# Moving two of sixteen attention numerators from a gate/up phase into the down phases

## The chip, the cores and the metric

The kernel runs on one core of a Trainium2 chip. The metric is device microseconds of one execution, lower is better. Times are medians; ratios are the mean time of one kernel's fast runs over that of the other's fast runs of the same rounds on the same chip, so they are not quite the ratio of the medians quoted beside them. All runs were at a granted TensorE clock of 0.999 or 1.0. The time from a DMA's issue to its last completion signal is called its *landing*.

## The reference, cut to what matters

```python
g = sigmoid((x * gate_w).sum(-1, keepdims=True))          # x: 2048 tokens x 640
# linear attention, 32 heads of 20
num = einsum("bhqf,bhfd->bhqd", phi_q, kv)                # "numerator" and, beside it, den
den = einsum("bhqf,bhf->bhq", phi_q, z)[..., None] + 1e-6
a = (num / den).reshape(B, S, D) @ wo
# GEGLU feed-forward, 640 -> 1728 -> 640
b = (gelu(x @ w_gate) * (x @ w_up)) @ w_down
out = g * a + (1 - g) * b
```

## The kernel before

Tokens are cut into 4 blocks of 4 tiles of 128. After the attention state (kv, z) is built, TensorE runs these phases in this order: gate/up of blocks 0 and 1, down of block 0, gate/up 2, down 1, gate/up 3, down 2, down 3. Each tile t also needs a *numerator*, `num(t)`: 20 small matmuls of TensorE into PSUM banks 2 to 5, ten VectorE operations, an add on GpSimd, and a DMA transpose into `goT`. The down phase then multiplies `goT` by `wo` in the same accumulation as the feed-forward. Every operation names ("marks") what it reads and writes, and the kernel's own scheduler makes a later writer wait for the last marked reader.

```python
def num(self, t):
    for i in range(self.KD):                  # 20 matmuls, two row halves r run side by side
        for s in (0, 1):
            for r in (0, 1):
                bk, a, o0 = NBK + 2 * r + s, 64 * r, 3 * i * DB          # NBK = 2
                sc.op("pe", lambda e: e.matmul(self.bank(bk)[:, o0:o0 + w], ...), writes=[("ps", bk)], ...)
    rb = [("ps", NBK + k) for k in range(4)]  # each VectorE operation that reads a bank marks all four as read
    dve(lambda e: e.reciprocal(R(0), Dn[1]), rb, [key(0)], guard=old)
    # ... seven more small operations ...
    for s, dst in ((0, self.O1), (1, self.O2)):
        dve(lambda e, ...: e.tensor_tensor(o, V[s][:, :, :, 0:DH], f, ALU.mult), rb + [key(6 + s)], ...)   # L678
    sc.op("pool", ... Og = O1 + O2 ...)                                   # L680
    sc.dma("sp", lambda e: e.dma_start_transpose(self.goT[:, gs, :, :], self.Og[:, sl, :]), ...)   # L683

# one down phase: two pairs of tiles, 74 steps each; a step is two matmuls (L708) that run side by side
cs = list(range(NFC + 1 if opens else NFC)) + [NFC + 1 + k for k in range(KD)]   # hT chunks, then goT chunks

def first_nums(idx):                          # second block's gate/up phase
    if idx in (2, 5, 8, 11):
        self.num(idx // 3)
at = (12, 46, 80, 116)                        # steps of a down phase after which a numerator is put
gateups(0, state)
gateups(1, first_nums)
for b in range(self.NB):
    downs(b, {at[k]: 4 * b + 4 + k for k in range(4)} if b < 3 else {})
    if b < 2:
        gateups(b + 2, none)
```

A pair needs its `goT` for the first time in step 15 of its 74, so the second pair of a phase needs it in step 89 of the phase.

The softmax here doesn't subtract the row's maximum and nothing guards it: scores larger than these inputs give would overflow.

Of the kernel before, what the change touches and what calls it, by code (L numbers as in the profile page):

```python
# [107 lines left out]
class _Kernel:  # L108
# [641 lines left out]
    def ffn(self):  # L750
        self.gn = 0
        self.pn = 0
        pairs = [(0, 1), (6, 7)]

        def gateups(b, after):
            for idx, c in enumerate([0, 1, 13] + list(range(2, 13))):
                self.gateup(b, c, pairs[self.pn % 2])
                self.pn += 1
                after(idx)

        def downs(b, side):
            p = [pairs[(self.pn + k) % 2] for k in (0, 1)]
            n = 0
            for t in (4 * b, 4 * b + 2):
                final = t + 2 == self.NT
                for _ in self.down_pair(t, p + [(2, 3)] if final else p, (256, 256, 128) if final else (320, 320)):
                    n += 1
                    if n in side:
                        self.num(side[n])

        def state(idx):
            if idx < 3:
                self.gram(13 + idx)
            if idx == 2:
                self.columns = False
                self.kv_evac()
                self.gates()
                self.kv_ones()
            if 6 <= idx < 11:
                self.kv_mask(idx - 6)  # L780

        def first_nums(idx):
            if idx in (2, 5, 8, 11):
                self.num(idx // 3)

        def none(idx):
            pass
        at = (12, 46, 80, 116)
        gateups(0, state)
        gateups(1, first_nums)  # L790
        for b in range(self.NB):
            downs(b, {at[k]: 4 * b + 4 + k for k in range(4)} if b < 3 else {})
            if b < 2:
                gateups(b + 2, none)

# [43 lines left out]
```

## Time and profile before

The kernel before took 289.85 us median of six runs (289.48 to 290.26).

| reading | number | where it is read |
|---|---|---|
| span | 288.7 us | page |
| TensorE busy | 98% of the span | page |
| chain that ended last | 97% TensorE | page |
| longest TensorE or weight-load wait after 86 us | under 0.5 us | waits |

The page's first part, busy time, share of the span and instructions of each engine:

```profile
PE 284.0 (98%) x3032; PEld 190.1 (66%) x3032; DVE 166.7 (58%) x337; ACT 105.1 (36%) x199; POOL 27.6 (10%) x52
```

From 86 us on the chain that ended last is an unbroken row of matmuls. These are pieces of it (start, length, what). First the gate/up stretches, without numerators and then with the first two of the second block's four; after the dots, the beginning of the second down phase:

```profile
86.32 29.24 PE ps L351 x135
115.56 0.50 PE ps L651 x20
116.06 6.67 PE ps L351 x30
122.73 0.50 PE ps L651 x20
123.23 6.58 PE ps L351 x30
...
192.93 1.74 PE ps L708 x24
194.67 0.39 PE ps L651 x20
195.06 4.62 PE ps L708 x68
```

Read: L351 is a gate or up matmul, 29.24/135 = 0.2166 us each, L651 a numerator's matmul, L708 a down matmul. Thirty L351 should take 6.50 us and take 6.58 to 6.67 after a numerator, so in gate/up a numerator costs its own 0.50 and about 0.1 more; in a down phase it costs about 0.4.

The timeline of the third down phase shows two numerators in a row and the room between them (start, length, engine, line, what; in brackets the idle time before and who ended it):

```profile
245.53 0.56 PE L651 MATMUL ps<-KV,Eq 64*128 64x88 bf16 x20
246.28 0.36 DVE L667 RECIPROCAL RH<-ps 128x32 f32<-128x32 f32 x1 [1.59 <-PE ps L651]
248.34 1.55 DVE L678 TENSOR_TENSOR O<-ps,RH 128x640 bf16<-128x640 f32 x2
250.02 1.39 POOL L680 TENSOR_TENSOR Og<-O,O 128x640 bf16<-128x640 bf16 x1 [34.32 <-DVE O L678]
250.40 0.55 PEld L651 LDWEIGHTS ps<-KV,Eq 64*128 64x128 bf16 x20
```

Read: the first numerator's matmuls begin at 245.53, VectorE reads the banks until 248.34 + 1.55 = 249.89, and the next numerator's weights load at 250.40 with no idle time in front. There is 0.5 us to spare.

### The profile page before, as it was taken

What the parts mean: (1) busy time and instruction counts of PE and PEld (TensorE: products, weight loads), DVE (VectorE), ACT (ScalarE), POOL (GpSimd) and SP (SyncE); (2) the same over time, 40 slices, a digit from 0 to 9 for tenths busy, and PEclk for the clock granted to TensorE, in tenths of its full rate; (3) what the DMA queues carried; (4) which work ended last, traced back from release to release, by engine and by line L of the source; (5) the groups of instructions that cost most, each with busy time, mean ns of one, the idle gap of its engine ahead of it and who ended that gap; (6) DMA issues with size and microseconds to landing.
All of it is one profiled execution on the core that took longest, in us unless ns stands there. A gap on an engine that the chain in (4) does not pass through costs nothing.

```text
span 288.7 us, 7036 instructions
## 1 busy us (share of the span) xinstructions
PE 284.0 (98%) x3032; PEld 190.1 (66%) x3032; DVE 166.7 (58%) x337; ACT 105.1 (36%) x199; POOL 27.6 (10%) x52
## 2 busy tenths in 40 slices
PE   7999999999999999999999999999999999999996
PEld 4576689999994444444688744457764444777785
DVE  2338999999977553777776443326744232674001
ACT  2357897687663322322111332220132222022111
POOL 7000000000000000111113200001230000113000
DMA  8999994000002000011212120000312000031211
GB/s 225 217 192 293 361 356 119 0 2 2 0 2 48 0 0 0 3 25 31 25 37 70 28 66 0 3 0 15 80 25 68 0 2 0 2 92 26 70 49 49
DMA packets 36938, 18.68 MB, mean 65 GB/s; under 512 B 28970, under 2 KB 36394, under 8 KB 36906
## 3 DMA queue, kind: packets, MB, share of 16 engines
q1 hardware_dynamic: 36096, 17.86, 23.8%
q8 instruction: 24, 0.39, 0.6%
q10 hardware_dynamic: 810, 0.35, 0.5%
q14 instruction: 8, 0.07, 0.1%
HBM read 9.04 MB, written 2.62 MB: 40 GB/s over the span
## 4 chain that ended last, share of the span: by engine, by line
PE 97%; DMA 1%; ACT 1%; issue 0%; ACTq 0%
PE ps L351 61%; PE ps L708 28%; PE ps L651 2%; PE ps L363 2%; PE ps L449 2%; DMA xtok<-in_A_x_dram 1%; PE ps L331 1%; PE ps L290 1%; ACT Ek L413 0%; ACT Eq L518 0%; ACT outsb L721 0%; ACT gcol L416 0%; PE ps L313 0%; ACTq L42 0%
## 5 line engine op out<-in xcount | busy, mean ns | idle before, releaser
L708 PE MATMUL ps<-wd_sb,hT 64*128 64x320 bf16 (+2 forms) x918 | 67.6, 288 | 0.0
L625 DVE TENSOR_TENSOR hT<-ps,gl 128x512 bf16<-128x512 f32 x52 | 35.7, 690 | 55.1 <-PE ps L351 54.9
L351 PE MATMUL ps<-xT,wg_sb 128*128 128x512 bf16 (+1 forms) x270 | 64.9, 379 | 0.0
L351 PE MATMUL ps<-xT,wu_sb 128*128 128x512 bf16 (+1 forms) x270 | 64.8, 379 | 0.0
L623 ACT ACTIVATE gl<-ps 128x512 bf16<-128x512 f32 x52 | 30.9, 597 | 71.5 <-PE ps L351 64.9
L708 PEld LDWEIGHTS ps<-wd_sb,hT 64*128 64x128 bf16 x918 | 46.0, 94 | 13.2 <-ACT gl L623 0.8
L351 PEld LDWEIGHTS ps<-xT,wu_sb 128*128 128x128 bf16 (+1 forms) x270 | 26.5, 99 | 29.7 <-DVE hT L625 0.4
L680 POOL TENSOR_TENSOR Og<-O,O 128x640 bf16<-128x640 bf16 x16 | 22.3, 1395 | 237.3 <-DVE O L678 237.3
L351 PEld LDWEIGHTS ps<-xT,wg_sb 128*128 128x128 bf16 (+1 forms) x270 | 25.9, 99 | 28.7 <-issue 0.5
L351 PE MATMUL ps<-w,xT 128*64 128x512 bf16 (+6 forms) x400 | 42.1, 325 | 0.0
L721 ACT ACTIVATE outsb<-ps,Gm 128x320 bf16<-128x320 f32 (+2 forms) x31 | 14.6, 516 | 74.8 <-PE ps L708 74.8
L351 PEld LDWEIGHTS ps<-w,xT 128*64 128x64 bf16 (+1 forms) x400 | 35.9, 107 | 4.7
L708 PE MATMUL ps<-wo_sb,goT 64*128 64x320 bf16 (+2 forms) x340 | 28.2, 288 | 0.0
L351 PE MATMUL ps<-xT,wq 128*64 128x512 bf16 (+1 forms) x185 | 26.4, 380 | 0.3 <-ACT Eq L518 0.3
L433 DVE TENSOR_TENSOR Ek<-Ek,Dk 128x640 bf16<-128x640 bf16 x32 | 25.0, 821 | 0.5
L678 DVE TENSOR_TENSOR O<-ps,RH 128x640 bf16<-128x640 f32 x32 | 24.8, 815 | 0.0
L424 DVE TENSOR_REDUCE Dk<-Ek 128x64 f32<-128x1280 bf16 x16 | 23.7, 1478 | 0.2 <-ACT gcol L416 0.2
L518 ACT ACTIVATE Eq<-ps 128x512 bf16<-128x512 f32 x40 | 21.7, 604 | 1.1 <-PE ps L351 0.8
L413 ACT ACTIVATE Ek<-ps 128x640 bf16<-128x640 f32 x32 | 20.7, 702 | 3.5 <-PE ps L351 3.5
L708 PEld LDWEIGHTS ps<-wo_sb,goT 64*128 64x128 bf16 x340 | 17.7, 94 | 4.7
L351 PEld LDWEIGHTS ps<-xT,wq 128*64 128x64 bf16 (+1 forms) x185 | 15.3, 108 | 3.5 <-ACT Eq L518 0.8
L667 DVE RECIPROCAL RH<-ps 128x32 f32<-128x32 f32 x16 | 5.7, 358 | 18.3 <-PE ps L651 18.3
(65 smaller groups left out, 151.1 us busy)
## 6 DMA issues: line engine op xcount, KB each, us to landing
out_dram<-outsb SPq DMA_DIRECT2D x7, 320.0 KB, 2.4
wd_sb<-in_B_w_down_dram SPq DMA_DIRECT2D x1, 2080.0 KB, 13.6
wg_sb<-in_B_w_gate_dram SPq DMA_DIRECT2D x1, 1120.0 KB, 6.0
wu_sb<-in_B_w_up_dram SPq DMA_DIRECT2D x1, 1120.0 KB, 8.5
wg_sb<-in_B_w_gate_dram SPq DMA_DIRECT2D x1, 960.0 KB, 9.7
wu_sb<-in_B_w_up_dram SPq DMA_DIRECT2D x1, 960.0 KB, 10.2
w<-in_A_wqkv_dram SPq DMA_DIRECT2D x5, 160.0 KB, 4.4
wo_sb<-in_A_wo_dram SPq DMA_DIRECT2D x1, 800.0 KB, 9.4
```

Of the source, the lines that this page charges most:

```text
L351: self.sc.op("pe", lambda e: e.matmul(self.ps[a:z, bank * 512 + c0:bank * 512 + c0 + n], lhs[:, a:z], rhs, start=first, stop=fin), reads=r ...
L363: sc.op("pe", lambda e, c0=c0, n=n, bk=bk, col=col: e.matmul(self.bank(bk)[:, col:col + n], self.xT[:, kt, t * P:(t + 1) * P], self.w3[:, ...
L413: self.sc.op("act", lambda e, s=s, scale=scale: e.activation(self.Ek[:, se, s, :], self.ps[:, o:o + self.D], AF.Exp, scale=scale), reads=[ ...
L424: sc.op("dve", lambda e: e.tensor_reduce(self.Dk[:, se, 0, :].rearrange("p (s h) -> p s h", h=H), self.Ek[:, se, :, :].rearrange("p s (h d ...
L433: sc.op("dve", lambda e, v=v, r=r: e.tensor_tensor(v, v, r, ALU.mult), reads=[("Rk", se)], writes=[("Ek", se, s)])
L518: sc.op("act", lambda e, s=s, scale=scale: e.activation(self.Eq[:, s, i, b * self.BT:(b + 1) * self.BT], self.bank(bank), AF.Exp, scale=sc ...
L623: sc.op("act", lambda e: e.activation(self.gl[:, slot, :], self.bank(banks[0]), AF.Gelu_apprx_tanh), reads=[("ps", banks[0])], writes=[("g ...
L625: sc.op("dve", lambda e: e.tensor_tensor(hT[:, c, :], self.bank(banks[1]), self.gl[:, slot, :], ALU.mult), reads=[("ps", banks[1]), ("gl", ...
L678: dve(lambda e, o=o, f=f, s=s: e.tensor_tensor(o, V[s][:, :, :, 0:DH], f, ALU.mult), rb + [key(6 + s)], [("O", s, sl)], guard=old)
L680: sc.op("pool", lambda e: e.tensor_tensor(self.Og[:, sl, :], self.O1[:, sl, :], self.O2[:, sl, :], ALU.add), reads=[("O", 0, sl), ("O", 1, ...
L708: sc.op("pe", lambda e: e.matmul(self.bank(bk, w), lhs, rhs, start=opens and x == 0, stop=end and not opens, skip_group_check=True), reads ...
L721: sc.op("act", lambda e: e.activation(dst, self.bank(bk, w), AF.Copy, scale=g), reads=rd, writes=wr)
```

## The change

The idea is that TensorE pays less for a numerator in a down phase than in a gate/up phase, so the second gate/up phase keeps only the two that block 0's first pair needs; each down phase then begins with the two of its own second pair.

```diff
         def first_nums(idx):
-            if idx in (2, 5, 8, 11):
-                self.num(idx // 3)
+            if idx in (4, 8):
+                self.num(idx // 4 - 1)
 ...
-        at = (12, 46, 80, 116)
+        at = (1, 29, 62, 98)
         gateups(0, state)
         gateups(1, first_nums)
         for b in range(self.NB):
-            downs(b, {at[k]: 4 * b + 4 + k for k in range(4)} if b < 3 else {})
+            downs(b, {at[k]: 4 * b + 2 + k for k in range(4 if b < 3 else 2)})
```

## The prediction

> **What bounds the kernel.** TensorE is busy 98% of the 288.7 us span and the chain that ended last is 97% TensorE, at full granted clock; every other engine is under 60%. In the waits view no PE or PEld wait after 86 us exceeds 0.5 us. Only TensorE time, or a new TensorE stall, can move the total.
>
> **What moves.** A "numerator" is 20 small matmuls into PSUM banks 2 to 5, then 10 VectorE operations, a GpSimd add and a DMA transpose into goT. There are 16 before and after. Before: 4 in the second gate/up phase, 4 in each of the first three down phases. After: 2, then 4, 4, 4, 2 by down phase.
> In the chain by time, the second gate/up stretch 115.56 to 141.81 is 26.25 us for 110 matmuls; without numerators 135 matmuls take 29.24, so 23.83 are matmuls and a numerator costs 0.605 us there. A down phase of 148 steps takes 21.78 us with 4 numerators; a pair without any takes 10.05, two 20.10: 0.42 us each. Moving two saves about 0.4 us of TensorE.
>
> **What it adds: two tight waits in each down phase.** By the timeline a down step is 0.136 us, VectorE starts 0.75 us after the numerator's first matmul, its chain lasts 3.61, GpSimd starts 0.13 later and lasts 1.40, the transpose lands 2.6 after its issue. (The Trainium skill, "Perfetto Trace Analysis", section "DMA Instruction — HWDGE": the profiled window leaves out the data movement; the trace agrees: windows of 1.2 us, landings 2.6 to 4.4.)
> 1. Banks 2 to 5. Before, numerators are 34 to 36 steps apart; now first and second are 28 apart: 28 x 0.136 + 0.42 = 4.22 us, while the banks are released 0.75 + 3.61 + about 0.05 = 4.4 us after the first's first matmul (all ten VectorE operations mark all four banks as read). With the lost weight prefetch a stall of 0.2 to 0.35 us in four down phases: about +1.0. The last gate/up product ends 0.8 us into the phase; the chain wants VectorE at 0.89, so it should not add.
> 2. The second numerator's goT. It starts 4.57 us into the phase and lands at 4.57 + 0.75 + 3.61 + 0.13 + 1.40 + 0.06 + 2.6 = 13.1. It is needed after step 88: 11.95 + 3 x 0.42 + 0.2 = 13.4 in the first three phases (fits), but 11.95 + 2 x 0.42 + 0.2 = 13.0, less 0.13 of prefetch, in the last: stall of 0.1 to 0.3.
> Steps 62 and 98 follow by 33 and 36 and fit.
>
> **Sum.** 289.78 - 0.4 + 1.0 + 0.2 = 290.6 us; 8 in 10: 289.4 to 292.0. Faster by over 2%: 1%, within 2%: 97%, slower: 2%.
>
> **What would show it.** Second gate/up phase shorter by 1.2 us. First three down phases longer by the stall alone, 0.2 to 0.35 each; the pause sits just before the second numerator, put down to VectorE's L678. Last down phase longer by 0.84 plus stalls, with a short pause before the second pair's wo matmuls, put down to the goT DMA. PE busy falls by 0.4, span rises.
>
> **What would make it wrong.** If VectorE releases the banks early enough, or TensorE's queue absorbs 0.2 us, the result is 289.4. If the last gate/up product delays the first chain, the stall grows and pushes the goT landing past its deadline too: +1 us per phase, 292 or more. A transpose that meets an output transfer landed in 4.4 us instead of 2.6; if the second numerator's does, +1.5 us per phase.

## The result, and the profile after

The changed kernel took 290.78 us median (290.03 to 291.05, 6 runs) against 289.85; the ratio is 1.0029, 95% interval 1.0014 to 1.0045. It is slower by 0.3%, well under the 2% line but clear of noise.

TensorE did a little less, yet the span grew:

```profile
PE 283.7 (98%) x3032; PEld 185.6 (64%) x3032; DVE 167.1 (58%) x337; ACT 105.0 (36%) x199; POOL 27.6 (10%) x52
```

After 86 us the waits view of the changed kernel has three lines for TensorE that the kernel before has not (engine, line, waited for: total us, times, longest):

```profile
PEld ps L708 <- DMA goT<-Og: 1.4, 2, 0.8
PEld ps L651 <- DVE O L678: 1.2, 3, 0.4
...
PE ps L708 <- DMA goT<-Og: 0.8, 2, 0.5
```

Now the chain's second gate/up stretch has only two numerators, and 40 or 50 matmuls between:

```profile
86.14 33.56 PE ps L351 x155
119.70 0.50 PE ps L651 x20
120.19 8.74 PE ps L351 x40
128.93 0.50 PE ps L651 x20
129.43 10.91 PE ps L351 x50
```

The third down phase's first two numerators, to be laid beside the lines of before:

```profile
242.89 0.69 DVE L625 TENSOR_TENSOR hT<-ps,gl 128x512 bf16<-128x512 f32 x1 [1.47 <-PE ps L351]
242.93 0.56 PE L651 MATMUL ps<-KV,Eq 64*128 64x88 bf16 x20
243.68 0.36 DVE L667 RECIPROCAL RH<-ps 128x32 f32<-128x32 f32 x1
245.75 1.55 DVE L678 TENSOR_TENSOR O<-ps,RH 128x640 bf16<-128x640 f32 x2
247.35 0.43 PEld L651 LDWEIGHTS ps<-KV,Eq 64*128 64x128 bf16 x20 [0.40 <-DVE O L678]
247.43 1.39 POOL L680 TENSOR_TENSOR Og<-O,O 128x640 bf16<-128x640 bf16 x1 [35.28 <-DVE O L678]
```

Read: the last gate/up product ends at 243.58 and VectorE begins the numerator at 243.68, 0.75 us after its first matmul, as predicted; it leaves the banks at 245.75 + 1.55 = 247.30, and only at 247.35 can TensorE load the second numerator's weights. The pause of 0.40 us is there in the first three down phases.

In the last down phase the two longest pauses are for `goT`, once before the first pair's `wo` matmuls and once before the second pair's. The first was not predicted:

```profile
263.44 1.21 SPq L683 DMA_TRANSPOSE goT<-Og  x1
...
267.74 0.52 PEld L708 LDWEIGHTS ps<-wo_sb,goT 64*128 64x128 bf16 x9 [0.78 <-DMA goT<-Og]
...
278.33 0.44 PEld L708 LDWEIGHTS ps<-wo_sb,goT 64*128 64x128 bf16 x9 [0.64 <-DMA goT<-Og]
```

The transpose issued at 263.44 is numerator 13's, the fourth of the third down phase; it landed 4.3 us after its issue, where most land in 2.6.

The loading at the start varies from run to run by more than the effects here: in fourteen traces the last group of attention-state matmuls began anywhere between 84.7 and 86.2 us, though of all edits only the 30 small matmuls of e6, e9, e10 and e12 come before it. Why it moves was not looked into. So the experiments are judged by the stretches behind it, which repeat to about 0.02 us where no pause varies. Stretch A runs from the start of the last group of attention-state matmuls to the first down matmul (it holds the first two gate/up phases), B and C from one down phase's start to the next one's, D from the third down phase's start to the end of the last matmul, as the timeline's starting times give them:

| us | A | B | C | D | sum | ratio of times to before, 95% interval |
|---|---|---|---|---|---|---|
| before | 55.99 | 51.13 | 51.01 | 42.04 | 200.17 | |
| after | 54.70 | 51.26 | 51.26 | 44.35 | 201.57 | 1.0029 (1.0014 to 1.0045) |
| e1_banks | 54.70 | 51.02 | 51.02 | 43.96 | 200.70 | 1.0021 (1.0006 to 1.0037) |
| e2_late | 54.70 | 51.25 | 51.26 | 44.10 | 201.31 | 1.0035 (1.0020 to 1.0050) |
| e3_both | 54.70 | 51.02 | 51.02 | 43.93 | 200.67 | 1.0013 (0.9999 to 1.0027) |
| e4_gap34 | 54.70 | 51.53 | 51.48 | 45.30 | 203.01 | 1.0087 (1.0071 to 1.0102) |
| e5_early | 54.69 | 51.02 | 51.02 | 43.32 | 200.05 | 0.9993 (0.9979 to 1.0007) |
| e6_fetch | 54.70 | 52.65 | 52.87 | 45.17 | 205.40 | 1.0187 (1.0171 to 1.0204) |
| e7_last1 | 54.70 | 51.02 | 51.02 | 42.82 | 199.56 | 0.9988 (0.9970 to 1.0006) |
| e8_marks | 54.70 | 51.26 | 51.26 | 44.53 | 201.75 | 1.0046 (1.0031 to 1.0061) |
| e9_before_fetch | 55.99 | 51.12 | 51.02 | 42.04 | 200.17 | 1.0003 (0.9985 to 1.0021) |
| e10_last1_fetch | 54.70 | 52.19 | 52.24 | 43.75 | 202.88 | 1.0071 (1.0042 to 1.0100) |
| e11_three | 55.31 | 51.02 | 51.02 | 42.43 | 199.78 | 0.9978 (0.9962 to 0.9995) |
| e12_three_fetch | 55.31 | 51.02 | 51.02 | 42.43 | 199.77 | 0.9996 (0.9979 to 1.0013) |

### The profile page after: what moved, and what is told of

Same layout as the page of the kernel before. It is cut to its first block, busy times and chain, and to the rows that moved or that the text cites. A ratio compares the mean times of both kernels' runs of the same rounds, so it can differ in the third digit from the quotient of the medians.

```text
span 289.8 us, 7035 instructions
## 1 busy us (share of the span) xinstructions
PE 283.7 (98%) x3032; PEld 185.6 (64%) x3032; DVE 167.1 (58%) x337; ACT 105.0 (36%) x199; POOL 27.6 (10%) x52
## 4 chain that ended last, share of the span: by engine, by line
PE 80%; DVE 6%; DMA 5%; SPq 4%; issue 1%; POOL 1%; ACT 1%; DVEq 0%; POOLq 0%; ACTq 0%
PE ps L351 58%; PE ps L708 18%; DMA wqT<-in_A_wqkv_dram 3%; DVE O L678 2%; DMA goT<-Og 2%; PE ps L651 2%; PE ps L449 2%; SPq L224 1%; SPq L220 1%; POOL Og L680 1%; SPq L233 1%; DVE hT L625 1%; DVE RH L667 1%; DVE RH L672 1%; PE ps L331 1%
## 5 line engine op out<-in xcount | busy, mean ns | idle before, releaser
L708 PEld LDWEIGHTS ps<-wd_sb,hT 64*128 64x128 bf16 x918 | 44.0, 94 | 15.1 <-ACT gl L623 0.8
L708 PE MATMUL ps<-wo_sb,goT 64*128 64x320 bf16 (+2 forms) x340 | 28.8, 288 | 0.8 <-DMA goT<-Og 0.8
L678 DVE TENSOR_TENSOR O<-ps,RH 128x640 bf16<-128x640 f32 x32 | 24.8, 817 | 0.0
L708 PEld LDWEIGHTS ps<-wo_sb,goT 64*128 64x128 bf16 x340 | 17.0, 94 | 7.0 <-DMA goT<-Og 1.4
```

Of the source, the lines that this page charges most:

```text
L678: dve(lambda e, o=o, f=f, s=s: e.tensor_tensor(o, V[s][:, :, :, 0:DH], f, ALU.mult), rb + [key(6 + s)], [("O", s, sl)], guard=old)
L708: sc.op("pe", lambda e: e.matmul(self.bank(bk, w), lhs, rhs, start=opens and x == 0, stop=end and not opens, skip_group_check=True), reads ...
```

## The experiments

All twelve gave correct results. Kernels ran beside fresh runs of the kernel before, whose medians were 289.35 (e1 to e4), 289.46 (e5 to e8), 289.24 (e9, e10) and 289.57 us (e11, e12).

**e1_banks: let the second numerator in earlier.** Against the changed kernel:

```diff
-        for i in range(self.KD):
-            for s in (0, 1):
+        for s in (0, 1):
+            for i in range(self.KD):
                 for r in (0, 1):
-                    bk, a, o0 = NBK + 2 * r + s, 64 * r, 3 * i * DB
+                    bk, a, o0 = NBK + 2 * s + r, 64 * r, 3 * i * DB
-        rb = [("ps", NBK + k) for k in range(4)]
+        rb = [[("ps", NBK + 2 * s), ("ps", NBK + 2 * s + 1)] for s in (0, 1)]
```

(Each VectorE operation that reads the banks takes `rb[0]` or `rb[1]`, whichever it reads, and N is viewed to match. The two banks of one sum were made neighbours so that a read of one sum spans no bank of the other.)

> The changed kernel, but a numerator's matmuls go sum by sum (all of the first two banks, then the other two), the two banks of one sum lie side by side, and each VectorE operation marks only the banks that it reads. So the first two banks are free 0.8 us before the other two. Theory (the pause of 0.40 us before the second numerator in the first three down phases is a true wait for banks 2 to 5, worth about 0.25 us each): the pauses put down to VectorE's L678 vanish, the first three down phases fall from 22.0 to about 21.8 us, the total falls by 0.6 to 0.8 us against the changed kernel, to about 290.1 (ratio to the kernel before about 1.001). The goT pauses of the last down phase (0.78 and 0.64 us) stay. Rival (the extra 0.25 us per phase is the price of putting a numerator at the first step, at the switch from gate/up to down): the pauses in the waits view may vanish, but the phases stay at 22.0 us and the total at 290.8.

Measured: 289.95 us against 289.35, ratio 1.0021. Against the changed kernel's 1.0029 that is no gain clear of noise; the trace decides. No pause is put down to L678 any more, and B and C fell from 51.26 to 51.02, 0.24 us each. The pause is a true wait for the banks; the rival is out. Both `goT` pauses stayed.

**e8_marks: the control to e1.** The order and place of e1, but the seven operations that read the banks mark all four again:

```diff
-        rb = [[("ps", NBK + 2 * s), ("ps", NBK + 2 * s + 1)] for s in (0, 1)]
+        rb = [[("ps", NBK + k) for k in range(4)]] * 2
```

> Control to e1: its order of matmuls and its place of the banks, but with the marks of the changed kernel (every VectorE operation marks all four banks). Theory (e1's gain came from the earlier release): the bank pauses of 0.3 to 0.4 us are back in the first three down phases, phases as in the changed kernel (51.26 us from one down phase's start to the next), total as the changed kernel, ratio about 1.003. Rival (e1's gain came from the order or the place): ratio about 1.002, phases 51.02.

Measured: 290.78 us against 289.46. Three pauses of up to 0.4 us for L678 are back, and B and C are 51.26 to the hundredth. So e1's gain in B and C is the earlier release and nothing else. (The prediction's "all ten" and the expectation's "every" count three operations too many, which read only `RH`; the last release is L678's either way.)

**e2_late: keep an output transfer away from numerator 13's transpose.** The output transfer of a phase's first pair is held back until after the fourth numerator:

```diff
-            sc.dma("sp", lambda e: e.dma_start(rows[:, :, c0:c1], ...), ...)
+            def send(): sc.dma("sp", lambda e: e.dma_start(rows[:, :, c0:c1], ...), ...)
+            if t0 % 4 == 0 and t0 < 12: self.held = send
+            else: send()
 ...
+                    if n == 100 and b < 3: self.held()
```

> The changed kernel, but the output transfer of the first pair of the first three down phases is issued after the fourth numerator's transpose, not before it. Theory (a transpose that is the first one after an output transfer lands in 4.0 to 4.4 us instead of 2.6; numerator 13 meets this and its goT holds up the last down phase's first pair): numerators 5, 9 and 13 now land in 2.6 us, the goT pause of 0.78 us in the last phase's first pair vanishes; in exchange the bank pause of about 0.25 us shows up there too, and the second goT pause stays at 0.3 to 0.6. Net: the last phase shorter by 0.3 to 0.6 us, total about 290.4. Rival (the late landing comes from something else, such as the position in the phase or the slot of goT): numerator 13 still lands in over 4 us and the total stays at 290.8.

Measured: 290.18 us against 289.35, ratio 1.0035, no better than the changed kernel's. With no output transfer in front of them, numerators 5, 9 and 13 still landed in 4.1, 4.4 and 4.1 us, and the `goT` pause stayed at 0.59. The theory fell: neighbourhood of an output transfer is not what makes a transpose late, though in the traces of before and after it had looked so.

**e3_both: e1 and e2 together.**

> Both edits. Theory: the two add, since they act on different waits: first three phases 21.8 us, last phase left with at most one goT pause before its second pair of about 0.2 us; total about 1.2 to 1.5 us under the changed kernel, 289.3 to 289.6, so at or a little under the kernel before (ratio 0.998 to 1.000): what is left is the 0.4 us of TensorE that the move saves. Rival (numerators in the last down phase cost more than 0.42 us for another reason than waits): the total stays at 290 or above though no pause is left in the waits view.

Measured: 289.56 us against 289.35, ratio 1.0013; expected 0.998 to 1.000. A miss, because only e1 acted: the stretches are e1's to 0.03 us. But its rival is not confirmed either, since both `goT` pauses (0.71 and 0.53 us) are still in the trace.

**e4_gap34: give the banks the room they had before.**

```diff
-        at = (1, 29, 62, 98)
+        at = (1, 34, 66, 100)
```

> The changed kernel with steps (1, 34, 66, 100) in place of (1, 29, 62, 98): first and second numerator 33 steps apart, as far as the kernel before has them. Theory (two limits pull against each other: banks want the second numerator late, its goT wants it early): no bank pause in any phase, but the second numerator's goT now lands at about 13.6 us into the phase against a need at about 13.1, so a goT pause of 0.4 to 0.5 us shows up before the second pair in each of the first three phases and of 0.8 to 0.9 in the last; total about 291.2 to 292, above the changed kernel. Rival (goT is ready in time with room, only the banks matter): total 290.0 to 290.3.

Measured: 291.85 us against 289.35. No bank pause, but five `goT` pauses, up to 1.3 us. B and C stand 0.51 and 0.46 us above e1's, which has no bank pause either. The step of the second numerator is caught between two limits, and the change had put it near the best place.

**What makes a transpose late.** The traces so far held the answer in the DMA view. This is that view of the changed kernel around numerator 13's transpose (window 263.4 to 267.8 us: busy tenths of the DMA engines in 40 slices of 0.11 us, then packets, MB and share by queue, then issues with KB and us to landing):

```profile
DMA  0000000000059999995500000000000499999997
q1 hardware_dynamic: 932, 0.49, 39.7%
q8 instruction: 1, 0.02, 1.2%
goT<-Og SPq DMA_TRANSPOSE x1, 4.3
```

and around numerator 15's, which landed in the usual time (window 275.6 to 278.6, slices of 0.075 us):

```profile
DMA  0000000000000000027999999998300000000369
q1 hardware_dynamic: 717, 0.22, 32.7%
goT<-Og SPq DMA_TRANSPOSE x1, 2.6
```

The two bursts of packets look alike: each starts about 1.2 us after the issue and lasts about 1 us. (What follows at the end of both windows is an output transfer.) What the late one has besides is one packet on q8, an instruction queue: 24 such packets in the whole run carry 0.39 MB, 16 KB each. The Trainium skill, page "Runtime: NRT & Kernel Launch", section "Instruction fetch mechanics", says what it is: each engine's instruction memory is refilled in blocks of 16 KiB, 256 instructions, over a DMA queue that the sequencer drives itself. And the page "DMA: Bandwidth & Descriptors", section "Issuing engines are not separate DMA queues", says that DMAs started by the scalar, sync or GpSimd engine run on the same 16 DMA engines and interleave. The packet size agrees with the trace, and the queue is TensorE's: from the first to the last of the 24 packets of the changed kernel 5890 weight loads and matmuls start, 256 to a packet. Whether the fetch really delays the transpose was open and was tested next.

**e5_early: move the fourth numerator out of the fetch's way.** On e1:

```diff
-        at = (1, 29, 62, 98)
+        at = (1, 29, 59, 88)
```

> e1 (narrow marks) with steps (1, 29, 59, 88) in place of (1, 29, 62, 98). In the traces so far every transpose that lands in over 2.7 us has a 16 KB transfer of the instruction queue 0 to 2.1 us after its issue, and no other has one. In e1 and e3 such a transfer falls about 2 us after numerator 13's issue. Theory (a fetch of instructions in the middle of the transpose holds up its last packets, and numerator 13's late landing of 4.2 us costs the first goT pause of the last phase): ten steps earlier the transpose is issued about 1.4 us before its old place, lands in 2.6 us with no fetch inside, the pause of 0.7 us in the last phase's first pair goes, and the second goT pause shrinks to 0.1 to 0.3 because numerator 15 no longer starts late. Last two phases 43.95 to about 43.2 us, total 0.6 to 0.8 under e1: ratio to the kernel before about 0.999 to 1.000. Rival (the fourth numerator of a phase lands late because of its place in the order): it still lands in over 4 us, though the pause may shrink as it is issued earlier.

Measured: 289.05 us against 289.46, ratio 0.9993. Numerator 13's transpose landed in 2.6 us, the pause in the last phase's first pair is gone, the second is 0.5 us (0.1 to 0.3 expected: a miss, explained below), and D fell from 43.96 to 43.32. That speaks for the fetch, but a numerator issued ten steps earlier could also have been saved by its place.

**e6_fetch: move the fetches and nothing else.** The changed kernel, with 30 tiny matmuls at the start, where TensorE waits for its input:

```diff
         warm(7)
+        for i in range(30):
+            sc.op("pe", lambda e: e.matmul(self.bank(0, 64), self.zero[:, 0:P], self.zero[:, 0:64], ...), ...)
```

> The changed kernel with 30 tiny matmuls on zeros at the start, where TensorE waits for its first input anyway: nothing else moves, but every later fetch of TensorE's instructions comes about 60 instructions sooner, which is about 2 us in a down phase. Theory (fetches make transposes land late): the fetch at 265.4 us moves to about 263.4, numerator 13's transpose, issued at about the same point, is no longer hit in its data phase and lands in 2.6 to 3.1 us; the first goT pause of 0.78 us falls to 0 to 0.3; other transposes may be hit instead, as the new fetch times say. Last two phases 44.35 to 43.7 to 44.0 us. Rival (landing depends on place, slot or the output transfer before it): landings as in the changed kernel, 4.0 to 4.4 for the fourth numerators, and last two phases at 44.35.

Measured: 294.90 us against 289.46 (4 fast runs), ratio 1.0187; the interval reaches over the 2% line, so the verdict against the kernel before is "unclear", though slower by far more than noise. Sixty TensorE instructions that do nothing useful cost about 1.5% against the changed kernel (1.0187 over 1.0029 is 1.016; over e8's 1.0046 from the same chip, whose stretches are almost the changed kernel's, 1.014). The fetches moved, and the late landings moved with them (issue and start of the fetch's packet in us from the start of the span; in brackets how long after the issue; "none": no packet within 2.6 us):

| numerator | after: issue | fetch | landing | e6: issue | fetch | landing |
|---|---|---|---|---|---|---|
| 3 (second of its phase) | 150.8 | none | 2.6 | 151.5 | 153.5 (+2.0) | 4.2 |
| 5 (fourth) | 161.0 | 162.6 (+1.6) | 4.0 | 163.0 | none | 2.6 |
| 7 (second) | 202.1 | none | 2.6 | 204.1 | 206.1 (+2.0) | 4.4 |
| 9 (fourth) | 212.2 | 214.2 (+2.0) | 4.1 | 215.9 | none | 2.6 |
| 11 (second) | 253.3 | none | 2.6 | 257.0 | 258.9 (+1.9) | 4.1 |
| 13 (fourth) | 263.4 | 265.5 (+2.1) | 4.3 | 268.4 | none | 2.6 |

Numerator 13 is cured, as expected, and D's first pause is gone; but now the second numerators are hit, the ones that have next to no room. The expectation named this possibility without its size: four `goT` pauses, B and C longer than the changed kernel's by 1.39 and 1.61 us. D, which holds numerator 11's pause, came to 45.17, not to the 43.7 to 44.0 expected. This is how one looks, the DMA view (window 256.9 to 261.2) and the timeline of e6, whose lines are numbered three higher:

```profile
DMA  0000000000005999999500000000000000000000
q8 instruction: 1, 0.02, 1.5%
goT<-Og SPq DMA_TRANSPOSE x1, 4.1
```

```profile
261.18 0.52 PEld L711 LDWEIGHTS ps<-wo_sb,goT 64*128 64x128 bf16 x9 [1.37 <-DMA goT<-Og]
```

Over all fourteen traces there are 224 of these transposes. By the packets' exact starts, in 68 of them a q8 packet starts 0.15 to 2.2 us after the issue: they landed in 2.8 to 4.5 us, and the 27 with the packet at 1.4 us or later all in 4.0 to 4.5. Of the other 156, 150 landed in 2.5 to 2.9 us; the six that took 4.3 to 4.5 had the packet 2.2 to 2.5 us after the issue, just at the end of the burst, where six others landed in 2.6.

The packets' times also show how the delay comes about. These are lines of e6's DMA view for numerator 11 (issued at 257.01), in the windows 258.9 to 259.9, 259.14 to 259.9 and 259.9 to 261.1:

```profile
q8 instruction: 1, 0.02, 6.4%
DMA packets 0, 0.00 MB, mean 0 GB/s; under 512 B 0, under 2 KB 0, under 8 KB 0
q1 hardware_dynamic: 2, 0.00, 0.2%
```

Read: the fetch is one packet that takes 6.4% of 16 engines' 1.0 us, so 1.02 us of one engine; it starts at 258.93 and ends at 259.95. The burst is over by 259.14, but for two last packets of the transpose, and these start at 259.94 and 259.95, when the fetch ends. So it is in all 33 late cases with the fetch at 1.4 us or later: 2 to 23 of the transpose's 672 packets start only at the fetch's end or after it. In the six that landed in 2.6 us none was left when the fetch came.

**e9_before_fetch: the same 30 matmuls in the kernel before.**

> Control to e6: the kernel before with the same 30 tiny matmuls at the start. Theory (the fetches cost e6 its time only because the changed kernel needs its second numerators' goT 0.3 us after they land): here each goT has most of a phase of room, so late landings, where they occur, hold up nothing: only the matmuls' own price at the start is seen, 0.4 to 0.8 us over the kernel before, ratio 1.0015 to 1.003, and phases as before (51.0 to 51.1 us from one down phase's start to the next). Rival (the tiny matmuls or the moved fetches slow TensorE itself): ratio near 1.015 as in e6.

Measured: 289.34 us against 289.24. All four stretches are the kernel before's to 0.01 us, though three transposes landed late (2.9 to 3.4 us). The kernel before itself is the stronger case: in its trace numerators 6, 10 and 14 landed in 4.1 to 4.4 us, and no wait for `goT` shows, since each `goT` landed 7.7 us or more before its first use. The 30 matmuls themselves cost less than expected, nothing that these runs can show. So neither they nor the moved fetches slow TensorE here; only a consumer without room pays.

**e7_last1: no tight place in the last phase.** On e1:

```diff
-        at = (1, 29, 62, 98)
+        at = (1, 29, 58, 87, 116)
-            downs(b, {at[k]: 4 * b + 2 + k for k in range(4 if b < 3 else 2)})
+            downs(b, {at[k]: 4 * b + 2 + k for k in range((4, 4, 5)[b])} if b < 3 else {1: 15})
```

> Narrow marks as in e1; numerators 2, 4, 4, 5, 1 by phase: the third down phase takes five (steps 1, 29, 58, 87, 116), the last one only number 15 at its first step. Theory: no tight wait is left at all (number 13 issued about 1.4 us earlier, number 14 a phase ahead, number 15 88 steps ahead), so only the TensorE saving of the move is left: last two phases about 42.04 + 0.84 = 42.9 us, total about 0.4 us under the kernel before, ratio 0.998 to 0.9995. Rival (numerators in the last phases cost more than 0.42 us of TensorE): ratio 1.000 or above with no pause in the waits view.

Measured: 288.85 us against 289.46, ratio 0.9988, with an interval that holds 1. No pause for the banks or `goT` is left in the waits view, and the sum is 199.56, 0.61 under the kernel before. This is what moving two numerators is worth to TensorE when nothing waits.

**e10_last1_fetch: e7 with the 30 matmuls.**

> e7 with the 30 tiny matmuls: how much of e7's result is luck of where the fetches fall. The second numerator of the first three phases still lands only about 0.2 us before it is needed, so if a fetch falls 1 to 2.1 us after its issue, as in e6, it lands in about 4.2 us and the phase grows by about 1.3 to 1.6. Theory: that happens in three phases, total 4 to 5.5 us over e7, ratio to the kernel before 1.014 to 1.019. Rival (in e7's order there is room): ratio 1.001 to 1.003.

Measured: 291.84 us against 289.24, ratio 1.0071. The direction is the theory's (numerators 3, 7 and 11 landed in 4.4, 4.5 and 4.2 us, three `goT` pauses), the size was put too high: B and C grew by 1.17 and 1.22 and D by 0.93 over e7's, not by 1.3 to 1.6, and the ratio expected was 1.014 to 1.019. The likely reason, not tested, is that the theory had taken e6's stalls without allowing that e7's second numerators start earlier by e1's 0.24 us. One of the six runs took 289.70, 1.4 us less than the next; there is no trace of it, so why is open. So e7's result rested on where the fetches happen to fall.

**e11_three: half of the change, with room.** The gate/up phase keeps three; each down phase begins with only one numerator of its own second pair:

```diff
-            if idx in (4, 8):
-                self.num(idx // 4 - 1)
+            if idx in (3, 6, 9):
+                self.num(idx // 3 - 1)
-        at = (1, 29, 62, 98)
+        at = (1, 36, 71, 106)
-            downs(b, {at[k]: 4 * b + 2 + k for k in range(4 if b < 3 else 2)})
+            downs(b, {at[k]: 4 * b + 3 + k for k in range(4 if b < 3 else 1)})
```

> Half of the change: one numerator moved, none in a tight place. Numerators 3, 4, 4, 4, 1 by phase, steps (1, 36, 71, 106); each down phase begins with the last one of its own second pair, wide marks as in the kernel before. Theory: no bank pause (35 steps apart) and no goT pause (the one numerator used in its own phase is issued 87 steps, about 12.5 us, before it is needed; it takes 8.5, or 10.3 with a fetch in it), so only TensorE's saving is left, 0.2 to 0.35 us: gram to end 199.8 to 200.0 us in the trace against 200.17, ratio 0.998 to 1.000. Rival (the first step of a down phase is itself a dear place): phases longer than 51.0 us, sum above 200.2.

Measured: 288.83 us against 289.57, ratio 0.9978, interval 0.9962 to 0.9995. No pause for banks or `goT`; sum 199.78, 0.39 under the kernel before. Three transposes landed in 4.2 to 4.5 us and held up nothing. It is the only version whose whole interval lies under the kernel before, and it needs no change to `num`. The gain is 0.2%.

**e12_three_fetch: e11 with the 30 matmuls.**

> e11 with the 30 tiny matmuls. Theory: with room before each goT, moved fetches change nothing: gram to end within 0.1 us of e11, ratio within 0.001 of it. Rival: a goT pause shows up and the sum grows by 1 us or more, as in e6 and e10.

Measured: 289.46 us against 289.57, ratio 0.9996 (0.9979 to 1.0013). In the trace the stretches are e11's to 0.01 us and no pause shows, as expected; the ratio lies 0.0018 above e11's, more than the 0.001 expected, but the two intervals overlap widely. By the trace e11 does not mind this move of the fetches; but as a time, its gain of 0.2% was not seen again.

## Why the prediction was right, point by point

The total was right (290.6 predicted, 290.78 measured), and so was the sign: TensorE saves less than the new waits take. Its terms were less even, and that the total came so close is in part luck: the saving was 0.2 us larger and the bank pauses 0.3 smaller than predicted, the `goT` pauses 1.1 larger. In the trace the sum of the stretches grew by 1.40 us (the median by 0.93; the rest was not traced to a place; the start of the run alone varies by about 1.5 us between traces).

- **TensorE's saving: predicted 0.4, measured about 0.6 us.** A shrank by 1.29 (predicted 1.2), and e7, which has no pause, stands 0.61 under the kernel before: the last phases of e7 pay 42.82 - 42.04 = 0.78 for two numerators, 0.39 each instead of 0.42, and B shrank by 0.11 for a reason that was not looked into.
- **The bank pause: predicted four times 0.2 to 0.35 us, measured three times 0.24 us** (B and C of after and e8 against e1; the third is in D and taken to be alike). The place, the releaser and the mechanism were right. The fourth is missing because in the last phase the unpredicted `goT` pause of the first pair comes before the second numerator and gives VectorE the time: in e6, where that pause is gone, there are four bank pauses (0.37 to 0.40 us each).
- **The claim that the last gate/up product does not delay the chain was right**, by 0.1 us: it ends at 243.58 and the chain starts at 243.68.
- **`goT`: predicted 0.1 to 0.3 us, in one pause; measured about 1.3 us, in two** (0.45 and 0.36 us of idle matmul time, 0.78 and 0.64 of idle weight loading). This is the term that was mis-sized: D of after less D of e7 is 1.53, and less one bank pause of 0.24 it is 1.29. The sentence that failed is "Steps 62 and 98 follow by 33 and 36 and fit." It looked at the banks, and did not hold numerator 13's `goT` against the last phase, which follows with no gate/up phase between. From that numerator's first matmul to its use lie 64 steps and two numerators, 64 x 0.136 + 2 x 0.42 = 9.5 us, less the 0.13 by which TensorE loads weights ahead of a matmul; its `goT` takes 8.55 us with a landing of 2.6, which fits, but 10.25 with the 4.3 measured. The second pause was larger than predicted for another reason: its deadline was counted as 88 steps of 0.136 us, but the last 14 of these are steps of the very last pair, with 256 columns, and take 1.53 us (276.16 to 277.69) and not 14 x 0.136 = 1.90. So `goT` is needed 0.37 us earlier. That the first pause made numerator 15 start late is not the reason: in e5 and e6, which have no first pause, the second is still 0.50 and 0.56 us.
- **"A transpose that meets an output transfer landed in 4.4 us" named the wrong cause.** e2 took the output transfer away and the landing stayed; e6 moved the instruction fetches and the landing moved. But the size of the danger was right: "if the second numerator's does, +1.5 us per phase" is what e6 then showed, 1.39 and 1.61.

So the 0.9 us come out as -0.61 of saving, +0.72 of bank pauses and +1.29 of `goT` pauses in the trace, 1.40 in sum, of which the timed runs show 0.93. (The `goT` term is what is left of D, so the three add up by construction.) What stays open: the whole of the delay. For numerator 11 in e6 the last packets come 0.8 us late, at the fetch's end, but the landing comes 1.5 us late; the other 0.7 us, after the last packet, has no explanation here. Nor does the trace name a packet's DMA engine: that fetch and last packets share one is inferred from the packets' times.

## What to carry to other kernels

When work is moved into a phase so that its result is used in the same phase, write down for each piece the latest moment at which its result is needed, in every phase and also across the border to the next one, and compare it with the slowest landing in the trace, not the median. A DMA that feeds TensorE within a microsecond of room can be made late by something as remote as 60 instructions at the start of the program; half of the moved work, with 2.5 us of room or more (e11), shows no pause with either of the two placings of the fetches that were tried. If a version is faster by a few tenths of a per cent, shift its instruction stream a little and time it again, to see whether it is the order or the luck.

## What the Trainium skill lacked or had wrong

- "Runtime: NRT & Kernel Launch", section "Instruction fetch mechanics", gives the cost of crossing a 16 KiB block as "mostly hidden". For TensorE itself that held here (e9: all stretches unchanged with the fetches moved). It lacks that a fetch in the middle of another DMA delays that DMA: SBUF-to-SBUF transposes landed in 2.8 to 4.5 us with a fetch 0.15 to 2.2 us after their issue (68 of 68), against 2.5 to 2.9 otherwise (150 of 156; the six exceptions had a fetch at 2.2 to 2.5 us), and one kernel lost about 1.5% when the fetches moved (e6). A fetch's packet takes 0.9 us or more, and the transpose's last packets start when it ends.
- No page says how long a DMA transpose of one 128 x 640 bf16 tile within SBUF takes to land; here 2.6 us, of which the sequencer's window is 1.2 ("Perfetto Trace Analysis", section "DMA Instruction — HWDGE", rightly says that the window leaves out the data movement).
- "DMA: Bandwidth & Descriptors", section "Issuing engines are not separate DMA queues", names the scalar, sync and GpSimd engines as issuers that share the 16 DMA engines; TensorE's instruction queue (here 24 packets of 16 KB) belongs in that list, by the packets' times: in 33 of 33 late transposes with the fetch at 1.4 us or later, the last packets start only when the fetch ends.
